# Eleven weight blocks widened in eleven chosen attention turns and five in the first dense batch; the last two token tiles finished in turn

## The chip, the cores and the metric

The kernel runs on one core of a Trainium2 chip. The metric is the device time of one execution in microseconds (us); a run's figure is the median of several executions. The engines are TensorE (PE, with its weight loads listed as PEld), VectorE (DVE), ScalarE (ACT), GpSimd (POOL) and SyncE (SP). SP issues nearly all DMA transfers, in the order of its queue.

## What is computed

An attention with a learned relative bias, then a mixing layer (two Fourier transforms), a normalization and a feed-forward layer with a residual. Shapes: 4 batches, 8 heads, 576 positions, head size 64; model size 512, hidden size 2048.

```python
scores = scale * np.matmul(q, k.transpose(0, 1, 3, 2)) + bias     # bias from a small MLP on |i - j|
attn = softmax(scores)
x = np.matmul(attn, v)                      # (4, 576, 512) after the heads are joined
mixed = np.real(np.fft.fft(np.fft.fft(x, axis=1), axis=2))
u = x + mixed
un = (u - mean(u)) / np.sqrt(var(u) + 1e-6)
out = u + np.maximum(un @ w_ch1, 0.0) @ w_ch2   # w_ch1: 512 x 2048, w_ch2: 2048 x 512
```

`w_ch1` and `w_ch2` arrive as 64-bit floats, seen by the kernel as 64-bit integers (`m1`, `m2`). The kernel makes them 32-bit itself.

## The kernel before

**Stages.** First the bias table is computed and kept in DRAM (0 to about 66 us). Then come 16 units of attention, each a pair of heads of one batch, `n = 4 * pair + batch`. Unit n's steps are spread over the loop's turn n and its neighbours, by the written orders `SECOND` (turn 1) and `ORDER` (turns 0 and 2 to 14). The last turn, 15, runs in the written order `TAIL` together with the mixing and normalization of batch 0. In these stages PE, DVE and ACT execute in the written order (each scope of `manual_schedule` keeps its own order); POOL and SP are ordered by the scheduler's simulation. Then follow four dense batches of four token tiles each, and a last one with the two tiles that hold the leftover positions (`rest_tiles`). In the dense batches the simulation orders everything, but for DVE in the first, whose written order is held.

**A turn.** In the orders, S is a block of scores on PE, D the addition of the bias and the row's extreme on DVE (line 292), X the exponential on ACT (line 307), T a transpose on PE into one of two PSUM buffers (line 451), VT or vT its evacuation to `pt` on ACT or DVE (lines 431, 433), A the product with the values on PE (line 472; five for each unit). W0 to W3 and U0 to U3 are the steps that widen a block of `m1` and one of `m2`.

**Widening** (`widen`, lines 153 to 166). A block is 512 x 128 of `m1` or 128 x 512 of `m2`: 512 KB in 64 bits. Its transfer into `raw` is issued when the tile is made. Step 0 is an ACT copy with a scale (line 162), steps 1 to 3 are a mask and two shift-and-or on DVE (lines 163 to 165). Step 3 is followed by a store of the 256 KB result to DRAM (`w1_d`, `w2_d`; lines 562 and 563). `raw` of `m1` is in pool `rawp`, that of `m2` in `rawu`, one buffer each, so a block's transfer can begin when the block before it is done.

**Which block when.** `weights(n)` widens block n of both matrices in turn n, for n = 1 to 15. Block 0 is widened in eight quarter pieces of 128 x 128 (`first_weights`, pool `rawx`) in turns 4 to 11.

**Transfers around it.** SP also issues, for each turn, `kT` and `qT` two units ahead (line 188), `v` two units ahead (line 195), and in the turn before a new pair of heads (n = 3, 7, 11) the bias of the next pair (line 238, issued from `largest`).

**A dense batch** (`dense`). For each of 16 hidden blocks f: `layer(f)` splits the weights into two fp32r parts (high on ACT, low on POOL; lines 932 and 933), runs `up(f)` on PE (12 matmuls into `hp`), then the ReLU's high part `hh` on ACT (line 972) and its low part `hl` on DVE (line 973). `down(f - 1)` adds the products of `hh`, `hl` and the parts of `w2` to the accumulators `acc` (12 matmuls with four tiles; line 989). `w2_load(f)` (line 952) loads `w2_d[f]` into one of two buffers in each batch; the 16 tiles of `w1` are loaded once, in the first batch, and stay. `run` merges several lists of pieces by their relative position, `(i + 0.5) / len`. In the first batch `main` has 27 pieces (layers 2 to 15, and downs 1 to 13 between them) and `pcs`, the mixing and normalization of batch 1, has 41. `end` adds each tile's accumulator to it on DVE (line 995) and stores it (`store`, lines 1059 and 1115).

Of the kernel before, what the change touches and what calls it, by code (L numbers as in the profile page):

```python
# [9 lines left out]
F32 = mybir.dt.float32  # L10
# [9 lines left out]
DM, FF, HID = 512, 2048, 32  # L20
P = 128
# [5 lines left out]
NF = FF // P  # L27
# [4 lines left out]
HB = {"d": 8, "a": 6}  # L32
WHO = "ddda"

FIRST = range(4, 12)
NEED = [0, 1, 3, 2]
N0 = 572
NT0 = N0 + S
# [92 lines left out]
def body(ctx, tc, a, out):  # L131
    nc = tc.nc
# [16 lines left out]
    w2_d = dram.tile([NF, P, DM], F32, name="w2_d")  # L149
# [264 lines left out]
    with ExitStack() as st:  # L414
# [1 line left out]
        otp = pool("otp", 2, stack=late, side="right")  # L416
        prp = pool("prp", 2, stack=late, side="right")
        rawu = pool("rawu", 1, stack=late, side="right")
        rawx = pool("rawx", 1, stack=late, side="right")
        tps = pool("tps", 2, PSUM, stack=st)  # L420
        ops = pool("ops", 1, PSUM, stack=st)
        score_ps = ExitStack()
# [117 lines left out]
        def turn_of(n, between):  # L540

            for i, w in enumerate(SECOND if n == 1 else ORDER):
                w, u = w.rstrip("'"), n - w.count("'")
                if w[0] in "WU":
                    if n:
                        wd(w)
                elif 0 <= u < U and (u or n == 1 or w[0] not in "SDX"):
                    steps[w[0]](u, w)
                for piece in between.pop(i, ()):
                    piece()  # L550
            assert not between
# [17 lines left out]
                    todo[4]()  # L569
            return step  # L570

        def first_weights(i):

            c = slice(P * (i % 4), P * (i % 4) + P)
            wf = rawx.tile([P, P], F32, tag="wf", name="wx")
            if i < 4:
                res = widen(a["m1"][c, 0:P], wf, [P, P], rawx)
                dst = w1_d[0][:, i]
            else:
                res = widen(a["m2"][0:P, c], wf, [P, P], rawx)  # L580
                dst = w2_d[0][:, c]
            last = res.pop()

            def end():
                last()
                nc.sync.dma_start(dst, wf)
            return res + [end]

        for n in range(U - 1):
            pr = prep(n + 1) if n else []  # L590
            if n:
                wd = weights(n)
            between = {4 + 8 * i: [piece] for i, piece in enumerate(pr)}
            if n in FIRST:
                for i, piece in zip((10, 30, 40, 50), first_weights(FIRST.index(n))):
                    between[i] = [piece]
            turn_of(n, between)
            if n + 2 < U:
                load(n + 2)
            if n == 0:  # L600
                while later:
                    keep_bias()
                x = xp.tile([P, B, 5, DM], F32, tag="x", name="x")
            if n == 6:
                fs = tabp.tile([P, 3, 2, 2, NK], F32R, tag="tab", name="fs")
                nc.gpsimd.tensor_copy(fs[0:1, 0, 0, 0, 0:1], vt[6][0:1, 0, 0:1])
                nc.gpsimd.dma_start(fs, a["fs"])
# [210 lines left out]
            return ut, across, high, low  # L818

        n = U - 1  # L820
        wd = weights(n)
        mix = Mix(0)
        tl = [x[:, 0, t] for t in range(4)]
        un, stats, root, scale = norm(tl)
# [93 lines left out]
        wsp = pool("wsp", 2, stack=st)  # L918
        fgp = pool("fgp", 1, stack=st)
        w1p = pool("w1p", 1, stack=st)  # L920
        hp_ = pool("hhp", 3, stack=st)
        w2p = pool("w2p", 2, stack=st)
        w1 = [w1p.tile([P, 4 * P], F32, name=f"w1_{i}") for i in range(NF)]
        w1 = w1[6:] + w1[:6]
# [11 lines left out]
        def dense(ut, tiles, store, n_first=0, mix=None):  # L936
# [45 lines left out]
                up(f)  # L982
                relu_parts(f)

            def down(f):
                h, w = hs.pop(f), w2s.pop(f)
                for t in range(n):
                    for k, (i, j) in enumerate(PROD):
                        nc.tensor.matmul(  # L989
                            acc[t], h[i][:, P * t:P * t + P], w[j],  # L990
                            start=f == 0 and k == 0, stop=f == NF - 1 and k == 2)

            def end():
                for t in range(n):
                    nc.vector.tensor_tensor(tiles[t], acc[t], tiles[t], ALU.add)
                    store(t)

            if n_first:
                for f in range(1, NF):
                    w1_load(f)  # L1000
                    if f < 3:
                        w2_load(f - 1)
                w1_load(0)
                part = lambda i: mix.fold(nc.vector, 0, i)
                for step, i in (
                        (w1_parts, 1), (part, 0), (part, 1), (relu_parts, 0), (w2_parts, 0), (part, 2),
                        (mix.fold_hi, 0), (w1_parts, 2), (up, 1), (mix.fold_lo, 0), (relu_parts, 1), (w2_parts, 1),
                        (down, 0)):
                    step(i)
                fixed.close()  # L1010
            pieces = []
            for f in range(n_first, NF):
                pieces.append(lambda f=f: layer(f))
                if 0 < f < NF - 1:
                    pieces.append(lambda f=f: down(f - 1))
            return pieces, [lambda: down(NF - 2), lambda: down(NF - 1)], end

        def run(*streams):
            order = []
# [22 lines left out]
        for b in range(B):  # L1042
# [8 lines left out]
            with ExitStack() as held:  # L1051
                if b == 0:
                    held.enter_context(tc.manual_schedule(engines={DVE_}))
                run(main, pcs)
            run(fl + last_down)
            end()

# [2 lines left out]

        main, last_down, end = dense(ut, rest_tiles, store)
        run(main)
        run(last_down)
        end()


def host_layout(inputs):
# [52 lines left out]
```

## Time and profile before

| | |
|---|---|
| median of 3 runs | 777.1 us (773.5 to 778.18) |
| profiled execution | 776.84 us, of which the span from first to last instruction is 775.1 us |
| mean granted TensorE clock | 0.998 |
| PE | 750.3 us busy, 97% of the span |
| DVE | 433.8 us, 56% |
| ACT | 435.2 us, 56% |
| POOL | 340.6 us, 44% |
| DMA | 103.49 MB moved, 134 GB/s on average |

Busy time is the time between the starts and ends of an engine's instructions; matmuls overlap, and their ends are modelled. An idle time in front of an instruction carries the name of what ended it. The chain of waits is followed back from the last instruction, at each step to what released it. Times in rows are us from the start of the span, unless a column says ns.

### The profile page before, as it was taken

What the parts mean: (1) busy time and instruction counts of PE and PEld (TensorE: products, weight loads), DVE (VectorE), ACT (ScalarE), POOL (GpSimd) and SP (SyncE); (2) the same over time, 40 slices, a digit from 0 to 9 for tenths busy, and PEclk for the clock granted to TensorE, in tenths of its full rate; (3) what the DMA queues carried; (4) which work ended last, traced back from release to release, by engine and by line L of the source; (5) the groups of instructions that cost most, each with busy time, mean ns of one, the idle gap of its engine ahead of it and who ended that gap; (6) DMA issues with size and microseconds to landing.
All of it is one profiled execution on the core that took longest, in us unless ns stands there. A gap on an engine that the chain in (4) does not pass through costs nothing.

```text
span 775.1 us, 13211 instructions
## 1 busy us (share of the span) xinstructions
PE 750.3 (97%) x4779; PEld 614.0 (79%) x4779; DVE 433.8 (56%) x968; ACT 435.2 (56%) x901; POOL 340.6 (44%) x290
## 2 busy tenths in 40 slices
PE   6999898999999999999999999999999999999997
PEld 4567686878777887878888888888888888888896
DVE  7997786887788787892843623513137141111443
ACT  7996886878888888653432433334333343333453
POOL 0003555564455663125455434544355444444442
PEclk9999999999999999999999999999999999999999
DMA  8988989989979862244211211122111222111332
GB/s 218 240 225 228 256 234 258 285 238 263 269 196 240 258 187 96 64 154 168 52 35 51 94 43 41 41 55 87 50 41 41 55 75 62 55 41 55 123 96 68
DMA packets 59793, 103.49 MB, mean 134 GB/s; under 512 B 8944, under 2 KB 29040, under 8 KB 58608
## 3 DMA queue, kind: packets, MB, share of 16 engines
q1 hardware_dynamic: 58976, 99.25, 45.5%
q0 software_dynamic: 288, 3.08, 1.3%
q8 instruction: 37, 0.61, 0.3%
q10 hardware_dynamic: 464, 0.33, 0.1%
q14 instruction: 28, 0.23, 0.1%
HBM read 78.90 MB, written 21.07 MB: 129 GB/s over the span
## 4 chain that ended last, share of the span: by engine, by line
PE 85%; DMA 5%; DVE 4%; ACT 4%; issue 1%; ACTq 0%; DVEq 0%; SPq 0%
PE acc L989 25%; PE hp L964 25%; PE s L271 10%; PE o L472 9%; PE t L451 6%; PE bps L400 3%; PE zp L684 2%; DMA raw<-m 2%; DMA bias<-ring 2%; PE abp L704 1%; DVE p L292 1%; ACT p L307 1%; PE ut L807 1%; DMA v<-v 1%; DVE hd L380 1%
## 5 line engine op out<-in xcount | busy, mean ns | idle before, releaser
L973 DVE SCALAR_TENSOR_TENSOR hl<-hp,hh 128x512 fp32r<-128x512 f32 (+1 forms) x80 | 50.9, 636 | 231.6 <-ACT hh L972 231.6
L964 PE MATMUL hp<-tok,w1h 128*128 128x512 f32 (+1 forms) x632 | 179.6, 368 | 0.0
L933 POOL TENSOR_TENSOR w1l<-w,w1h 128x512 fp32r<-128x512 f32 x79 | 103.1, 1305 | 111.9 <-ACT w1h L932 110.7
L964 PEld LDWEIGHTS hp<-tok,w1h 128*128 128x128 f32 x632 | 115.0, 188 | 20.1
L933 POOL TENSOR_TENSOR w2l<-w2f,w2h 128x512 fp32r<-128x512 f32 x64 | 84.1, 1315 | 106.5 <-ACT w2h L932 106.3
L292 DVE CUSTOM_DVE_ANT_0 p<-s,bias 128x576 f32<-128x576 f32 x128 | 95.3, 753 | 39.4 <-PE s L271 35.9
L964 PE MATMUL hp<-tok,w1l 128*128 128x512 f32 (+1 forms) x316 | 116.1, 368 | 0.0
L932 ACT ACTIVATE w2h<-w2f 128x512 fp32r<-128x512 f32 x80 | 50.5, 631 | 116.5 <-POOL w1l L933 79.7
L989 PE MATMUL acc<-w2h,hh 128*128 128x512 f32 x288 | 112.4, 390 | 0.0
L989 PE MATMUL acc<-w2l,hh 128*128 128x512 f32 x288 | 112.4, 390 | 0.0
L932 ACT ACTIVATE w1h<-w 128x512 fp32r<-128x512 f32 x79 | 49.8, 631 | 111.3 <-PE hp L964 102.8
L989 PE MATMUL acc<-w2h,hl 128*128 128x512 f32 x288 | 107.6, 391 | 0.0
L271 PE MATMUL s<-kh,qs 128*128 128x288 f32 (+1 forms) x320 | 98.3, 326 | 4.0 <-DVE nm L292 3.9
L307 ACT ACTIVATE p<-p,nm 128x576 f32<-128x576 f32 x128 | 98.0, 771 | 1.4 <-DVE nm L292 1.4
L431 ACT ACTIVATE pt<-t 128x512 f32<-128x512 f32 x141 | 77.6, 594 | 32.6 <-PE t L451 19.5
L271 PE MATMUL s<-kl,qs 128*128 128x288 f32 (+1 forms) x320 | 88.2, 295 | 0.9 <-DVE kl L212 0.9
L451 PE MATMUL t<-ident,p 128*128 128x128 f32 x576 | 79.1, 273 | 6.5 <-ACT pt L431 6.5
L208 POOL TENSOR_SCALAR kh<-kT 128x576 fp32r<-128x576 f32 (+1 forms) x28 | 22.4, 819 | 141.5 <-PE s L271 113.7
L472 PE MATMUL o<-pt,v 128*64 128x288 f32 x640 | 84.2, 411 | 0.0
L271 PEld LDWEIGHTS s<-kh,qs 128*128 128x128 f32 (+1 forms) x320 | 58.5, 183 | 20.7 <-issue 7.0
L451 PEld LDWEIGHTS t<-ident,p 128*128 128x128 f32 x576 | 66.2, 140 | 8.1 <-ACT pt L431 7.7
L472 PEld LDWEIGHTS o<-pt,v 128*64 128x64 f32 x640 | 43.3, 137 | 30.7 <-issue 4.7
(149 smaller groups left out, 1276.2 us busy)
## 6 DMA issues: line engine op xcount, KB each, us to landing
w2f<-w_d SPq DMA_DIRECT2D x80, 256.0 KB, 2.7
raw<-m SPq DMA_DIRECT2D x30, 512.0 KB, 5.5
kT<-kT SPq DMA_DIRECT2D x32, 304.0 KB, 5.7
qT<-qT SPq DMA_DIRECT2D x32, 288.0 KB, 5.0
bias_d<-ring SPq DMA_DIRECT2D x54, 144.0 KB, 2.7
bias<-bias_d SPq DMA_DIRECT2D x24, 288.0 KB, 6.1
v<-v SPq DMA_DIRECT2D x16, 320.0 KB, 7.0
out<-x SPq DMA_DIRECT2D x18, 256.0 KB, 3.2
```

Source lines behind the costliest of these rows:

```text
L271: nc.tensor.matmul(ps[:m, c, :CH], qs[:, c0:c0 + m], kk[:, k0 + c * CH:k0 + (c + 1) * CH], start=k == 0, stop=k == 1, skip_group_check=True)
L292: nc.vector.tensor_tensor_reduce(p, bank.pop((n, i))[:, :, :CH], bias, -0.125, 3.0e38, ALU.add, ALU.min, nms[n][:, blk:blk + 1])
L307: nc.scalar.activation(p, p, AF.Exp, bias=nms[n][:, blk:blk + 1], scale=-1.0, accum_out=sums[n][:, blk:blk + 1])
L400: nc.tensor.matmul(ps[32 * t4:32 * t4 + 32, c, :CH], w2[:, int(rev)], h[:, c * CH:(c + 1) * CH], start=True, stop=True, tile_position=(0, ...
L431: nc.scalar.activation(dst, src, AF.Copy)
L451: nc.tensor.transpose(tp[:, 128 * t:128 * t + 128], pb[t].rearrange("p h s -> p (h s)")[:, k0:k0 + 128], ident)
L472: nc.tensor.matmul(os_[u][e, c, :CH], vt[u][:, j, e], pts[u][:, 2 * j + h if j < 4 else 8, c * CH:(c + 1) * CH], start=j == 0, stop=j == 4 ...
L932: nc.scalar.activation(h, src, AF.Copy)
L933: eng.tensor_tensor(l, src, h.bitcast(F32), ALU.subtract)
L964: nc.tensor.matmul(ps[:, :N], w[wi][:, P * kb:P * kb + P], ut[ui][:, kb, :N], start=i == 0, stop=i == len(mm) - 1)
L973: nc.vector.scalar_tensor_tensor(hl[:, :N], ps[:, :N], 0.0, hh[:, :N].bitcast(F32), ALU.max, ALU.subtract)
L989: nc.tensor.matmul(acc[t], h[i][:, P * t:P * t + P], w[j], start=f == 0 and k == 0, stop=f == NF - 1 and k == 2)
```

## The change

- Eleven blocks (0 to 10) are widened in turns 2, 3, 5, 6, 7, 9, 10, 11, 13, 14 and 15: turn n takes block `WIDE.index(n)`. Turns 1, 4, 8 and 12 have no weight work. `first_weights` and its pool go.
- Blocks 11 to 15 are widened in the first dense batch by `widen_rest`: ten half blocks, each of four pieces (start the transfer; ACT copy and mask; shift-and-or; shift-and-or, and for `m2` the store to `w2_d`), merged into the batch as a third list of 44 places (40 pieces and four empty ones at its end). The transfers of the first two half blocks come first; half block k + 2 starts when half block k is done. An `m1` block is widened straight into its `w1` tile, so that no store and no load are needed for it.
- The pool of `hh` and `hl` has two buffers instead of three; a pool `rawd` for the `m2` blocks is new.
- In the last batch, the two hidden blocks at the end are applied to tile 0 first, which is added and stored, and then to tile 1.

```diff
--- before.py
+++ after.py
@@ -32,7 +32,7 @@
 HB = {"d": 8, "a": 6}
 WHO = "ddda"
 
-FIRST = range(4, 12)
+WIDE = [2, 3, 5, 6, 7, 9, 10, 11, 13, 14, 15]
 NEED = [0, 1, 3, 2]
 N0 = 572
 NT0 = N0 + S
@@ -416,7 +416,6 @@
         otp = pool("otp", 2, stack=late, side="right")
         prp = pool("prp", 2, stack=late, side="right")
         rawu = pool("rawu", 1, stack=late, side="right")
-        rawx = pool("rawx", 1, stack=late, side="right")
         tps = pool("tps", 2, PSUM, stack=st)
         ops = pool("ops", 1, PSUM, stack=st)
         score_ps = ExitStack()
@@ -542,7 +541,7 @@
             for i, w in enumerate(SECOND if n == 1 else ORDER):
                 w, u = w.rstrip("'"), n - w.count("'")
                 if w[0] in "WU":
-                    if n:
+                    if n in WIDE:
                         wd(w)
                 elif 0 <= u < U and (u or n == 1 or w[0] not in "SDX"):
                     steps[w[0]](u, w)
@@ -569,31 +568,11 @@
                     todo[4]()
             return step
 
-        def first_weights(i):
-
-            c = slice(P * (i % 4), P * (i % 4) + P)
-            wf = rawx.tile([P, P], F32, tag="wf", name="wx")
-            if i < 4:
-                res = widen(a["m1"][c, 0:P], wf, [P, P], rawx)
-                dst = w1_d[0][:, i]
-            else:
-                res = widen(a["m2"][0:P, c], wf, [P, P], rawx)
-                dst = w2_d[0][:, c]
-            last = res.pop()
-
-            def end():
-                last()
-                nc.sync.dma_start(dst, wf)
-            return res + [end]
-
         for n in range(U - 1):
             pr = prep(n + 1) if n else []
-            if n:
-                wd = weights(n)
+            if n in WIDE:
+                wd = weights(WIDE.index(n))
             between = {4 + 8 * i: [piece] for i, piece in enumerate(pr)}
-            if n in FIRST:
-                for i, piece in zip((10, 30, 40, 50), first_weights(FIRST.index(n))):
-                    between[i] = [piece]
             turn_of(n, between)
             if n + 2 < U:
                 load(n + 2)
@@ -818,7 +797,7 @@
             return ut, across, high, low
 
         n = U - 1
-        wd = weights(n)
+        wd = weights(WIDE.index(n))
         mix = Mix(0)
         tl = [x[:, 0, t] for t in range(4)]
         un, stats, root, scale = norm(tl)
@@ -918,7 +897,8 @@
         wsp = pool("wsp", 2, stack=st)
         fgp = pool("fgp", 1, stack=st)
         w1p = pool("w1p", 1, stack=st)
-        hp_ = pool("hhp", 3, stack=st)
+        hp_ = pool("hhp", 2, stack=st)
+        rawd = pool("rawd", 1, stack=st)
         w2p = pool("w2p", 2, stack=st)
         w1 = [w1p.tile([P, 4 * P], F32, name=f"w1_{i}") for i in range(NF)]
         w1 = w1[6:] + w1[:6]
@@ -982,21 +962,21 @@
                 up(f)
                 relu_parts(f)
 
-            def down(f):
-                h, w = hs.pop(f), w2s.pop(f)
-                for t in range(n):
+            def down(f, tiles=None):
+                h, w = hs[f], w2s[f]
+                for t in range(n) if tiles is None else tiles:
                     for k, (i, j) in enumerate(PROD):
                         nc.tensor.matmul(
                             acc[t], h[i][:, P * t:P * t + P], w[j],
                             start=f == 0 and k == 0, stop=f == NF - 1 and k == 2)
 
-            def end():
-                for t in range(n):
+            def end(which=None):
+                for t in range(n) if which is None else which:
                     nc.vector.tensor_tensor(tiles[t], acc[t], tiles[t], ALU.add)
                     store(t)
 
             if n_first:
-                for f in range(1, NF):
+                for f in range(1, len(WIDE)):
                     w1_load(f)
                     if f < 3:
                         w2_load(f - 1)
@@ -1013,7 +993,37 @@
                 pieces.append(lambda f=f: layer(f))
                 if 0 < f < NF - 1:
                     pieces.append(lambda f=f: down(f - 1))
+            if n == 2:
+                return pieces, [lambda t=t, f=f: down(f, [t]) for t in range(2) for f in (NF - 2, NF - 1)], end
             return pieces, [lambda: down(NF - 2), lambda: down(NF - 1)], end
+
+        def widen_rest():
+
+            chunks = []
+            for f in range(len(WIDE), NF):
+                chunks.append(chunk(
+                    a["m1"][:, P * f:P * f + P].rearrange("(k p) c -> p k c", p=P), [P, 4, P], w1[f], f, rawp))
+                chunks.append(chunk(a["m2"][P * f:P * f + P], [P, DM], None, f, rawd))
+            res = [chunks[0].pop(0), chunks[1].pop(0)]
+            for k, c in enumerate(chunks):
+                res += c + [b.pop(0) for b in chunks[k + 2:k + 3]]
+            return res
+
+        def chunk(src, shape, dst, f, rp):
+            todo = []
+
+            def start():
+                wf = rp.tile([P, DM], F32, tag="wf", name="wf") if dst is None else dst
+                todo.extend(widen(src, wf, shape, rp))
+                if dst is None:
+                    todo.append(lambda: nc.sync.dma_start(w2_d[f], wf))
+
+            def step(*which):
+                for i in which:
+                    if i < len(todo):
+                        todo[i]()
+
+            return [start, lambda: step(0, 1), lambda: step(2), lambda: step(3, 4)]
 
         def run(*streams):
             order = []
@@ -1051,7 +1061,10 @@
             with ExitStack() as held:
                 if b == 0:
                     held.enter_context(tc.manual_schedule(engines={DVE_}))
-                run(main, pcs)
+                    wide = widen_rest()
+                    run(main, pcs, wide + [lambda: None] * (len(wide) // 10))
+                else:
+                    run(main, pcs)
             run(fl + last_down)
             end()
 
@@ -1060,8 +1073,9 @@
 
         main, last_down, end = dense(ut, rest_tiles, store)
         run(main)
-        run(last_down)
-        end()
+        for t in range(2):
+            run(last_down[2 * t:2 * t + 2])
+            end([t])
 
 
 def host_layout(inputs):
```

## Rows read from the trace of the kernel before

**Rows 1.** Windows, first dense batch: us, then each engine's busy us, PEclk, DMA share, GB/s
```profile
346.00:437.00 91.00, 91.00 (x436) 76.72 (x435) 45.09 (x78) 35.06 (x70) 47.37 (x38) 1.00 0.26 79
```

**Rows 2.** Timeline of PE: start, us, instruction; in brackets idle time before, what ended it
```profile
81.56 1.15 PE L451 MATMUL t<-ident,p 128*128 128x128 f32 x8 [2.50 <-ACT pt L431]
...
132.15 1.14 PE L451 MATMUL t<-ident,p 128*128 128x128 f32 x8 [2.48 <-ACT pt L431]
...
158.16 0.40 PE L271 MATMUL s<-kh,qs 128*128 128x288 f32 x1 [0.91 <-DVE nm L292]
...
198.88 1.14 PE L451 MATMUL t<-ident,p 128*128 128x128 f32 x8 [0.94 <-ACT pt L431]
```

**Rows 3.** The chain of waits in order of time: start, us, what
```profile
73.41 5.63 DMA raw<-m
...
114.45 4.03 PE o L472 x32
121.12 8.45 DMA raw<-m
133.29 4.03 PE o L472 x32
...
182.73 4.03 PE o L472 x32
190.80 6.09 DMA v<-v
200.02 4.03 PE o L472 x32
...
248.28 4.03 PE o L472 x32
...
280.46 4.03 PE o L472 x32
```

**Rows 4.** Timeline of ACT, turns 1 and 8
```profile
79.06 0.66 ACT L162 ACTIVATE uf<-raw 128x512 f32<-128x512 f32 x1 [3.86 <-DMA raw<-m]
...
196.35 0.68 ACT L162 ACTIVATE uf<-raw 128x512 f32<-128x512 f32 x1 [1.99 <-DMA raw<-m]
```

**Rows 5.** Groups by line and shape, 66 to 300 us: count, busy us, mean ns, idle before
```profile
L164 DVE SCALAR_TENSOR_TENSOR raw<-raw 128x512 int32<-128x512 int32 x28 | 23.1, 823 | 0.5
L163 DVE TENSOR_SCALAR raw<-raw 128x512 int32<-128x512 int32 x28 | 14.2, 506 | 9.0 <-ACT wf L162 9.0
L165 DVE SCALAR_TENSOR_TENSOR uf<-uf,raw 128x512 int32<-128x512 int32 x14 | 12.2, 868 | 0.5
...
L162 ACT ACTIVATE wf<-raw 128x512 f32<-128x512 f32 x14 | 9.3, 666 | 0.0
```

**Rows 6.** Timelines of DVE and PE in the first dense batch
```profile
363.49 0.69 DVE L973 SCALAR_TENSOR_TENSOR hl<-hp,hh 128x512 fp32r<-128x512 f32 x1 [3.22 <-ACT hh L972]
...
389.78 0.68 DVE L973 SCALAR_TENSOR_TENSOR hl<-hp,hh 128x512 fp32r<-128x512 f32 x1
...
367.81 0.39 PE L989 MATMUL acc<-w2h,hh 128*128 128x512 f32 x1
...
392.71 0.39 PE L989 MATMUL acc<-w2h,hh 128*128 128x512 f32 x1
```

**Rows 7.** Waits of SP's queue, 345 to 437 us: us in total, times, longest
```profile
SPq L952 <- POOL w2l L933: 73.8, 15, 6.8
```

**Rows 8.** DMA issues: count, KB, median us to landing; whole run, then 115 to 135 us
```profile
raw<-m SPq DMA_DIRECT2D x30, 512.0 KB, 5.5
...
raw<-m SPq DMA_DIRECT2D x3, 512.0 KB, 8.1
```

**Rows 9.** Timeline of the end, DVE and SP's queue
```profile
769.47 1.29 DVE L995 TENSOR_TENSOR x<-acc,x 128x512 f32<-128x512 f32 x2 [1.68 <-PE acc L989]
770.18 0.94 SPq L1059 DMA_DIRECT2D out<-x  x2
```

**Rows 10.** Line 933, 345 to 440 us: ns least/median/most, first and last start, form
```profile
L933 POOL TENSOR_TENSOR w2l<-w2f,w2h x17: 1282/1292/1987, 347.6 to 439.5; 128x512 fp32r<-128x512 f32 x17
```

## The prediction

> **What bounds the kernel now.** I read the row of busy time by stage first. In the first dense batch (346 to 437 us) TensorE is busy for all 91 us, while DVE is busy for 45.09, ACT for 35.06 and POOL for 47.37 [rows 1]. That stage, and the three batches behind it, are one unbroken stream of matmuls: nothing that ACT, DVE or POOL do there costs time until it makes TensorE wait.
>
> The attention stage comes before it, and there I looked for the rows of TensorE that have idle time in front. From 75 to 300 us there are six; the four longest are shown [rows 2]: 2.50, 2.48 and 0.94 us, each ended by ACT's copy of transposed scores, and 0.91 us ended by DVE. The other two are under 0.5 us each, and the change does not touch them.
>
> The chain of work says what that costs. A run of 32 `o` matmuls straddles the end of every turn, so the distance from one run to the next is a turn. Five turns (9 to 13) take 280.46 - 200.02 = 80.44 us, 16.09 us each. Turn 4 takes 133.29 - 114.45 = 18.84 us, 2.75 more; turn 8 takes 200.02 - 182.73 = 17.29 us, 1.20 more [rows 3]. The idle times there are 2.48 and 0.94 us, so a stall costs about 0.27 us beyond its idle row. In the same chain the weight transfers `raw` hold up the stall of turn 1 (5.63 us from 73.41) and of turn 4 (8.45 us from 121.12), and a transfer of `v`, issued just behind one, that of turn 8 (6.09 us from 190.80) [rows 3].
>
> ACT's rows close it: in turns 1 and 8 it sat for 3.86 and 1.99 us before the copy that opens a block (`uf<-raw`), waiting for `raw<-m` [rows 4]; turn 4 has the same picture. ACT works in order, so the exponentials and the evacuations behind that copy waited too, and TensorE ran out of free transpose banks. These are turns 1, 4 and 8; in turns 4 and 8 the queue also carries the bias of the next pair of heads.
>
> **The change part by part.**
>
> *Blocks leave turns 1, 4, 8 and 12.* With no weight copy in those turns, ACT has nothing there that waits for `raw`. Turn 4 should fall by 2.75 us and turn 8 by 1.20 us to 16.09. Turn 1's order of work differs, so I take its idle row plus the same 0.27: 2.77 us. Turn 12 shows no stall: 0. Sum 6.72 us. What is late next? The buffers of `raw` come free at the same moments as before, so the transfers for turns 2, 5 and 9 can start where those for turns 1, 4 and 8 did and have a turn more to land; `kT` and `v` then wait behind no more than before. I count no new wait; the price if one appears is a rival.
>
> *The eight quarter pieces of block 0 go from turns 4 to 11.* They take DVE, ACT and queue work out of turns that TensorE bounds. The five turns of 16.09 us hold three with such a piece (9 to 11) and two without (12, 13) [rows 3]; 248.28 - 200.02 and 280.46 - 248.28 both give 16.09 a turn. Worth 0. The 0.91 us of turn 6 [rows 2] come from DVE: two operations on a small column that belong to the tail's order were run in that turn. The change does not move them, so I leave that stall; the bounds are 0 and, by its turn's excess, 1.2 us of gain.
>
> *Five blocks go into the first dense batch.* Ten half blocks, each one ACT copy of 666 ns, one mask of 506 ns and two shift-and-or of 823 and 868 ns on DVE [rows 5]. Added: 10 x 0.67 = 6.7 us of ACT and 10 x 2.20 = 22.0 us of DVE. DVE goes from 45.1 to 67.1 and ACT from 35.1 to 41.8 of 91 us [rows 1]. Neither fills. The cover for single delays is the time between `hl` (the low part of the hidden layer) and the `acc` matmul run that needs it: 364.18 to 367.81 is 3.63 us, and the tightest steady case, 390.46 to 392.71, is 2.25 us [rows 6]. The pieces come one at a time, three to a layer, each under 0.9 us; alone they fit.
>
> The danger is DVE's fixed order in this batch. A mask that stands ahead of an `hl` waits for its ACT copy, the copy for its transfer, and `hl` and all the folds wait behind it. By the interleaving rule, a half block's transfer is issued five of 44 places ahead of its mask: 5 / 44 x 91 = 10.3 us. Against that: SP's queue is in order, and a `w2f` load at its head waits for POOL, 73.8 us in 15 waits, 4.9 on average and 6.8 at most [rows 7]; then `raw` takes 5.5 us to land (median of 30), 8.1 in the crowded turn 4 [rows 8]. Typical: 4.9 + 5.5 = 10.4, in balance with 10.3 and inside the 2.25 of cover. Worst: 6.8 + 8.1 = 14.9, over 12.6 by 2.3 us. The DMA engines are busy for 0.26 of this stage [rows 1], not crowded, so I take the typical end: 0 us, with 0 to 2.3 us for each of eight half blocks (the first two start early) as bounds. The 15 added transfers less five `w1` loads also stand in SP's queue; their issues are well under a microsecond each and come out of its waiting.
>
> *Hidden-layer buffers from three to two.* `up(f)` comes after `down(f-2)` on TensorE, so the buffer that the ReLU of layer f takes is free before its input exists: 0. If the scheduler put a ReLU ahead of that matmul, it would cost up to one `down`, 2.7 us, once for each batch.
>
> *The last two token tiles in turn.* Before, both final additions run after the last matmul, 769.47 to 770.76, and the second store follows the second one [rows 9]. Afterwards the first addition runs under the six matmuls of the other tile. What goes is the second's half of the 1.29 us, 0.65 us. The two issues take 0.94 us [rows 9], so the bounds are 0.3 (a first-tile product that waits for `hl`) and 0.94. I take 0.65.
>
> *POOL beside the added work.* POOL's `w2l` takes 1.29 us in the median of this stage and 1.99 us at the longest [rows 10], so something holds it up now and then. The Trainium skill (SBUF — State Buffer, "SBUF: two separate sides") says that a DVE operation with two SBUF inputs and a GpSimd operation that reads SBUF exclude each other for a whole instruction. The row agrees in direction. By that rule each of the 20 added shift-and-or operations could hold POOL for its full length; rival 3 gives what that would cost.
>
> **Sum.** 6.72 + 0.65 = 7.37 us off the profiled execution's 776.84 us: 769.5 us. The median before is 777.1, so the profiled execution stands for it within 0.3 us. One per cent, about what a measurement of this kernel can tell from no change, is 7.8 us: the bound lies at 769.3, almost on the forecast.
>
> **Rivals.**
> 1. *The transfers come late in the dense batch.* For: a queue whose head nearly always waits, and a fixed DVE order. Against: the balance above and idle DMA engines. One to three half blocks at about 2 us: 771.5 to 776.
> 2. *Slower.* The same mechanism on every half block, at the worst: 8 x 2.3 = 18.4 us, 788 us. It passes 1% slower (784.9) when each of the eight lands more than 1.9 us beyond the cover, 14.5 us after its buffer came free. Against it: it needs the longest queue wait and turn 4's landing time at once, each time.
> 3. *DVE shuts POOL out.* Each of the 20 added operations (0.85 us on average [rows 5]) holds POOL up for its length: 17 us, and 786.5 us if POOL had no slack. Against: POOL is busy for 47.37 of 91 us [rows 1], and 47.4 + 17 = 64 still leaves 27 us.
> 4. *A stall moves instead of going.* `kT`, `v` or a bias part is the next to be late in turn 4 or 8. For: the DMA engines stay crowded there, `raw` still taking 8.1 us to land [rows 8]. Half of 3.95 us comes back: 771.5.
> 5. *More gain.* Turn 6's 1.2 us goes too, or the end saves 0.94: 768 to 768.5.
>
> **How the numbers follow.** Forecast (stalls gone, batch hides the work) 0.60; rival 1 0.13; rival 2 0.05; rival 3 0.03; rival 4 0.07; rival 5 0.12. Rivals 2 and 3 hold the 0.08 for slower by over 1%. The forecast's case straddles the bound at 769.3, a little more of it above than below: 0.26 of its 0.60 counts as faster, and with rival 5 that is 0.38. The rest, 0.54, is within 1%. The range reaches down to rival 5 with a us for the spread of runs, 766.8, and up to most of rival 1, 775. The forecast's own range is 768.3 to 771.
>
> **What would show it.** In the profile after, right: the idle rows at turns 1, 4 and 8 are gone, those runs of `o` lie 16.1 us apart, the dense stage from its first matmul to its last is as long as before, and one addition stands after the last matmul. Wrong: idle rows on TensorE between 346 and 440 us; `hl` waiting for a mask that waits for `raw` (rivals 1 and 2); `w1l` or `w2l` well over 1.3 us with TensorE waiting for POOL (rival 3); an idle row in turn 4 or 8 ended by another transfer (rival 4).

## The result and the profile after

The kernel after takes 779.71 us in the median (777.77 to 782.89), the kernel before, run beside it, 775.3 us (773.5 to 779.57). The ratio is 1.0055, with an interval of 1.0039 to 1.0071. The change makes the kernel 0.55% slower: no difference by the bound of one per cent, yet on the other side of the forecast and above the range. The profiled execution is one of the slower ones of after, 781.77 us at a mean granted clock of 0.992; the three of the 17 at 0.999 or above took 777.77 to 778.46 us.

The profiled execution of after has a span of 779.8 us, 4.7 us more than before. I split it at the first `hp` matmul (line 863 after, 884 before) and at the last two `acc` matmuls (line 969, before 989): up to the first it is the attention with its tail, between the two the five dense batches.

| profiled execution | first `hp` | last two `acc` | dense stage |
|---|---|---|---|
| before | 343.26 | 769.04 | 425.78 |
| after | 339.43 | 774.98 | 435.55 |

The attention got 3.83 us shorter and the dense stage 9.77 us longer.

**Attention.** On TensorE's timeline after, the idle rows of turns 1, 4 and 8 [rows 2] are gone, and the runs of `o` around turn 4 lie 16.10 us apart where they lay 18.84 apart [rows 3]:

```profile
114.08 4.10 PE L471 MATMUL o<-pt,v 128*64 128x288 f32 x32
...
130.18 4.10 PE L471 MATMUL o<-pt,v 128*64 128x288 f32 x32
...
155.39 0.40 PE L271 MATMUL s<-kh,qs 128*128 128x288 f32 x1 [1.19 <-DVE nm L292]
```

The last row is turn 6's stall, left as forecast (1.19 us for 0.91). Nearly all that this profile lacks of the forecast 6.72 us it lost ahead of turn 1: an idle row of 1.55 us at 66.5 us (0.59 before), and behind it a granted TensorE clock of 0.52 and 0.63 from 68 to 72 us. Such a row comes and goes with the same work: it is 1.44 us in a kernel with the attention of before, and 0.52 to 1.87 us in the kernels with that of after. So it belongs to a run, not to the change.

**First dense batch.** The row of busy time by stage, as in [rows 1] (us; then PE, PEld, DVE, ACT, POOL; granted clock, DMA share, GB/s):

```profile
346.00:437.00 91.00, 87.56 (x403) 72.84 (x403) 64.30 (x98) 33.80 (x70) 46.11 (x35) 0.98 0.35 115
```

TensorE, busy for all 91 us before, is now busy for 87.56. DVE has 64.30 us, near the 67.1 of the sum, and ACT not even as much as before: neither is full. The waits view from 380 to 445 us (who waited for whom: us in total, times, longest) names whom TensorE waited for:

```profile
PE acc L969 <- ACT hh L952: 4.2, 2, 2.2
...
PE acc L969 <- DVE hl L953: 1.5, 1, 1.5
```

These are three idle rows: 1.46 us at 391.6, 1.97 at 418.2 and 2.20 at 442.8. ACT's timeline shows the copies that waited and what stood ahead of the last two `hh` (the high part of the hidden layer, line 952); the copy at 364.82 comes up again further below:

```profile
364.82 0.66 ACT L162 ACTIVATE w<-raw 128x512 f32<-128x512 f32 x1 [2.70 <-DMA raw<-m]
...
391.72 0.66 ACT L162 ACTIVATE wf<-raw 128x512 f32<-128x512 f32 x1 [4.99 <-DMA raw<-m]
...
399.82 0.69 ACT L162 ACTIVATE w<-raw 128x512 f32<-128x512 f32 x1 [4.87 <-DMA raw<-m]
...
407.21 0.66 ACT L162 ACTIVATE wf<-raw 128x512 f32<-128x512 f32 x1 [4.90 <-DMA raw<-m]
...
416.51 0.66 ACT L162 ACTIVATE w<-raw 128x512 f32<-128x512 f32 x1 [6.84 <-DMA raw<-m]
417.07 0.61 ACT L912 ACTIVATE w1h<-w 128x512 fp32r<-128x512 f32 x1
417.59 0.58 ACT L952 ACTIVATE hh<-hp 128x512 fp32r<-128x512 f32 x1
...
441.08 0.63 ACT L912 ACTIVATE w2h<-w2f 128x512 fp32r<-128x512 f32 x1 [6.30 <-DMA w2f<-w_d]
441.61 0.61 ACT L912 ACTIVATE w1h<-w 128x512 fp32r<-128x512 f32 x1
442.13 0.58 ACT L952 ACTIVATE hh<-hp 128x512 fp32r<-128x512 f32 x1
```

ACT waits at eight of the ten copies, 2.70 to 6.84 us each, and every one of these eight starts when its transfer lands. Behind the copy at 416.51 stand `w1h` and `hh`, then DVE's `hl`, then TensorE. The copy's transfer shows why it was late (SP's queue, then DVE's rows: an `hl`, the release of the buffer, the next `hl`):

```profile
412.71 0.38 SPq L160 DMA_DIRECT2D raw<-m  x1
...
408.91 0.69 DVE L953 SCALAR_TENSOR_TENSOR hl<-hp,hh 128x512 fp32r<-128x512 f32 x1 [4.46 <-ACT hh L952]
...
412.00 0.68 DVE L165 SCALAR_TENSOR_TENSOR w<-w,raw 128x512 int32<-128x512 int32 x1
418.20 0.69 DVE L953 SCALAR_TENSOR_TENSOR hl<-hp,hh 128x512 fp32r<-128x512 f32 x1 [5.52 <-ACT hh L952]
```

The transfer could be issued only when DVE had let go of the buffer, at 412.7. ACT had been at the copy since 416.51 - 6.84 = 409.67, 3 us before the issue. The transfer itself took 3.8 us, the median of the nine issued from 338 us on. DVE was late with the buffer because its `hl` at 408.91 had waited 4.46 us for the `hh` behind the copy at 407.21: a late copy makes the next transfer late too. The third stall has one more link: block 15 of `m2` is stored at 436.24 and loaded again from 438.28, and the `w2h` that waits for it stands ahead of `hh`. Counted from the first `hp`, that store comes at 96.81 us here and at 88.92 us in the kernel below with only two transfers: it comes late because DVE's work does by then.

Behind two of the stalls TensorE's clock fell too (2-us windows, columns as above):

```profile
416.00:418.00 2.00, 0.25 (x2) 0.00 (x0) 0.00 (x0) 1.49 (x3) 0.24 (x1) 1.00 0.20 76
418.00:420.00 2.00, 1.78 (x7) 1.46 (x8) 1.76 (x3) 1.70 (x4) 2.00 (x2) 0.91 0.00 0
420.00:422.00 2.00, 2.00 (x6) 1.51 (x6) 2.00 (x4) 0.00 (x0) 0.98 (x2) 0.50 0.00 0
422.00:424.00 2.00, 2.00 (x8) 1.62 (x7) 1.99 (x4) 0.64 (x1) 1.85 (x3) 0.74 0.19 69
```

0.50 is the lower of the two levels, 1.2 GHz. The missing clock of these windows is 2 x (0.09 + 0.50 + 0.26) = 1.70 us of work, and the third stall's windows give as much (0.88, 0.50, 0.76: 1.72). Idle 5.63 and clock 3.42 make 9.05 of the 9.77 us.

**The end.** The additions stand where they stood [rows 9]:

```profile
774.98 0.61 PE L969 MATMUL acc<-w2h,hl 128*128 128x512 f32 x2
775.40 1.29 DVE L975 TENSOR_TENSOR x<-acc,x 128x512 f32<-128x512 f32 x2 [1.68 <-PE acc L969]
776.12 0.94 SPq L1072 DMA_DIRECT2D out<-x  x2
```

The edit wrote the products tile by tile, but PE is not held to the written order in that batch, and the scheduler ran the last matmuls of both tiles in the old order.

### The profile page after: what moved, and what is told of

Its sections match the earlier page's. It is cut to its first block, busy times and chain, and to the rows that moved or that the text cites. A ratio compares the mean times of both kernels' runs of the same rounds, so it can differ in the third digit from the quotient of the medians.

```text
span 779.8 us, 13166 instructions
## 1 busy us (share of the span) xinstructions
PE 754.9 (97%) x4779; PEld 617.1 (79%) x4779; DVE 441.7 (57%) x950; ACT 434.8 (56%) x895; POOL 339.8 (44%) x290
## 5 line engine op out<-in xcount | busy, mean ns | idle before, releaser
L913 POOL TENSOR_TENSOR w2l<-w2f,w2h 128x512 fp32r<-128x512 f32 x64 | 86.0, 1343 | 108.2 <-ACT w2h L912 108.1
L208 POOL TENSOR_SCALAR kh<-kT 128x576 fp32r<-128x576 f32 (+1 forms) x28 | 20.6, 752 | 142.5 <-DMA bias_d<-ring 72.0
```

The costliest lines, as they stand in the source:

```text
L208: nc.gpsimd.tensor_scalar(dst[:, c], src[:, c], 1.0, 0.0, ALU.mult, ALU.add)
L913: eng.tensor_tensor(l, src, h.bitcast(F32), ALU.subtract)
```

## The experiments

Diffs are against the kernel after unless said otherwise. "Dense stage" is measured as in the table above. The kernel before took 775.2 to 775.6 us in all these comparisons.

### Taking the widening out of the batch, part by part

**No widening in the batch.**

```diff
-                    run(main, pcs, wide + [lambda: None] * (len(wide) // 10))
+                    run(main, pcs)
```

with all 16 blocks of both matrices loaded, from blocks `f % 11`.

> The changed kernel without the widening in the first dense batch: blocks 11 to 15 are not made at all, and the 32-bit blocks 0 to 4 are loaded a second time in their place, so the output is not the reference's. Attention, hidden-layer buffers and the end stay as changed. Theory T (the ACT copies of the half blocks stand in ACT's queue ahead of the ReLU's high part and wait there for transfers that are issued too late): the dense stage falls from 435.9 us back to the 426.2 us of before, and the time from 779.7 to about 770. Rival L (DVE has too much work in that batch): the same here, since that work is gone too. Rival B (the two hidden-layer buffers, or something in the attention, cost it): the dense stage stays several us above 426, the time above 775.

Measured: 768.95 us, ratio 0.9926 (0.9898 to 0.9955); first `hp` 335.88, dense stage 425.76 us, that of before, with two buffers for `hh` and `hl`. The attention edit alone is worth 6.2 us in the medians and 7.4 in the profile, where turn 6's stall happens to be missing. The chain of waits has 14 runs of `o`; ten of the 13 distances between them are 16.06 to 16.14 us, turn 4 among them (16.09); turn 8 takes 16.25 us:

```profile
112.04 4.03 PE o L471 x32
128.13 4.03 PE o L471 x32
...
176.44 4.03 PE o L471 x32
192.69 4.03 PE o L471 x32
```

**No ACT copy.**

```diff
-            return [start, lambda: step(0, 1), lambda: step(2), lambda: step(3, 4)]
+            return [start, lambda: step(1), lambda: step(2), lambda: step(3, 4)]
```

(the last shift-and-or reads the masked words in place of the copy's; not shown)

> The changed kernel without the ACT copy of the ten half blocks in the dense batch; the last shift-and-or reads the masked words in its place, so blocks 11 to 15 are wrong. Transfers, stores and all three DVE operations stay. Theory T: nothing on ACT waits for a transfer, so the waits for the ReLU's high part (4.2 us of idle on TensorE, and the drops of its clock that follow) go; what is left is what DVE's own waits cost: 771 to 775. Rival L: DVE does the same work, the time stays at 778 to 780.

Measured: 771.47 us, ratio 0.9945 (0.9921 to 0.9968); dense stage 427.02 us with one idle row, 0.97 us at 389 behind `hl`, and full clock.

**Two transfers instead of ten.** The first two half blocks are transferred, the other eight work on the same buffers.

```diff
-        raw = rp.tile(shape, I64, tag="raw", name="raw")
+        raw = kept.get(rp) if kept else None
+        if raw is None: ...   # tile and transfer, once for each pool
```

> The changed kernel in which only the first two half blocks of the dense batch are transferred; the other eight go through all their ACT, DVE and store work on the words that lie in the buffers, so blocks 12 to 15 are wrong. Theory T: no copy waits for a transfer, 770 to 772. Rival L: the work on DVE and ACT is all there, 777 to 780.

Measured: 769.03 us, ratio 0.9924 (0.9899 to 0.9948); dense stage 426.06 us. The same stretch as above:

```profile
346.00:437.00 91.00, 91.00 (x438) 76.56 (x437) 67.83 (x106) 38.58 (x76) 47.02 (x37) 1.00 0.23 70
```

All the widening work is there, DVE even 3.5 us busier than after, and TensorE is busy for all 91 us. So it is not the work; the transfers are needed for every one of the three stalls, also for the one that `hl` ends. This kernel takes away their traffic together with the waiting for them; the kernel without the ACT copy has all ten transfers and yet neither of the stalls that `hh` ends, so what those two need is ACT waiting for a transfer.

**The ten half blocks on top of the kernel before** (its attention and its buffers of block 0 untouched; `hhp` with two buffers, `rawd` and `widen_rest` added).

> The kernel before, with all its widening in the attention, and in the first dense batch the changed kernel's ten half blocks on top (blocks 11 to 15 are made twice), with its pools. If the dense batch alone carries the loss, about 775.3 + 9.8 = 785 us, whatever theory holds in the batch; if the loss comes from the two parts together, or from the attention, it stays under 780.

Measured: 782.66 us, ratio 1.0099 (1.0061 to 1.0136); dense stage 434.08 us with idle rows of 1.38 (`hl`), 2.14 and 2.27 us (`hh`) in the same places and one of 0.83 us (`hl`) at 439. The dense part alone brings a loss of 8.30 us in its stage; the time lies 2.3 us under the 785 expected.

### Moving the copy, the end of the list, ACT's order

**Copy on DVE.**

```diff
-            lambda: nc.scalar.activation(dst, hi.bitcast(F32), AF.Copy, scale=2.0 ** -112),
+            lambda: nc.vector.tensor_scalar(dst, hi.bitcast(F32), 2.0 ** -112, None, ALU.mult),
```

(in the dense batch only; the same with `nc.gpsimd` in the next one)

> The kernel after, with the scaling copy of the ten half blocks of the first dense batch done by DVE instead of ACT (one multiplication more on DVE for each, about 0.5 us by the shift-and-or rows; ten make 5 us of the 91). Theory T (the copies hold up ACT's order, and with it the high part of the hidden layer): ACT is free, and DVE, which waits for the mask anyway, waits as it did without any copy: 770 to 772.5 us, no idle row on TensorE ended by ACT, no lost clock in the dense stage, below the kernel before. Rival Q (any in-order engine that takes the copy gives the wait to TensorE, since the low part and the folds stand behind it on DVE): 777 us or more, with idle rows ended by DVE's low part.

Measured: 777.89 us, ratio 1.0031 (1.0014 to 1.0049). My theory missed by 5 us, and rival Q had the time, though not the instruction that ends the row. ACT's stall at 418 us is gone and one of 0.94 us is left at 441, but TensorE stood for 3.88 us before 391.28, ended by a fold of DVE (`z11l`), and its clock fell to 0.50 for about 6 us. DVE's rows from 380 to 396 us are back to back: folds of the mixing, widening and `hl`, without one idle time. In this stretch DVE has no room. The one copy that DVE does between 380 us and that fold takes 0.42 us, so its length does not explain 3.88 us. TensorE's order differs: here one `acc` matmul stands between the last `hp` and the product of that fold, in after there are eight. That this order is the rest of the 3.88 us was not tested.

**Copy on GpSimd.**

> The kernel after, with the copy of the ten half blocks of the first dense batch done by GpSimd. Theory T: ACT is free; GpSimd was busy for about half of this batch and its low parts of the weights have slack of some us, so 769 to 773 us. Rival Q: the wait of 3 to 5 us for a transfer now stands ahead of a low part of the weights (w1l, w2l), TensorE's idle rows are ended by POOL, and the time is 775 us or more.

Measured: 772.59 us, ratio 0.9967 (0.9945 to 0.999); dense stage 429.75 us, idle rows 2.10 us (`hl`, 390) and 1.31 us (`hh` behind the load of block 15, 436). This lies within the theory's 769 to 773.

**An earlier end of the list.**

```diff
-                    run(main, pcs, wide + [lambda: None] * (len(wide) // 10))
+                    run(main, pcs, wide + [lambda: None] * (len(wide) // 2))
```

> The kernel after, with 20 empty places at the end of the third list instead of 4: the widening ends at two thirds of the batch instead of nine tenths, and a transfer has fewer other pieces between its start and its copy. Theory T: less time for each transfer, so the copies wait longer on ACT and TensorE has at least as many idle rows: 779 to 786 us. Rival E (it is the late end: block 15 of the second matrix goes through a store and a load just before it is needed): that stall goes, and the time falls by what it costs with its lost clock, about 4 us, to 775 or 776 us.

Measured: 771.05 us, ratio 0.9941 (0.9919 to 0.9962). My expectation was wrong in direction, and the rival's too small. Five places between a transfer's start and its copy are 7.6 us here instead of 10.3, and ACT's waits did not get longer: 25.3 us in 8 against 35.9 in 9 (waits view, from 340 to 445 us; of after, then of this kernel).

```profile
ACT w L162 <- DMA raw<-m: 18.6, 4, 6.8
ACT wf L162 <- DMA raw<-m: 17.3, 5, 5.0
```
```profile
ACT wf L162 <- DMA raw<-m: 13.8, 4, 5.9
ACT w L162 <- DMA raw<-m: 11.5, 4, 3.6
```

So the lead by places says nothing about ACT's waits, and not every wait of ACT costs time: by these rows it counts which `hh` a copy stands ahead of. With the copies over by 409 us the stalls of 418 and 443 us are gone, two short ones are left (0.78 us by `hl` at 388, 1.25 by `hh` at 402), the clock stays at 1.00, and the dense stage takes 429.01 us.

**ACT held to the written order.**

```diff
-                    held.enter_context(tc.manual_schedule(engines={DVE_}))
+                    held.enter_context(tc.manual_schedule(engines={DVE_, ACT_}))
```

> The kernel after, with ACT as well as DVE held to the written order in the first dense batch. In the kernel after, ACT reached each copy of a half block before its transfer had landed, twice before it was even issued: the scheduler orders ACT by its own simulation. Theory O (the lead by written places exists, and the scheduler's order of ACT threw it away): the copies wait little, the high part of the hidden layer is in time, TensorE's idle rows ended by ACT between 380 and 440 us go but for the one of the last block's store and load (442 us), and the time is 771 to 774 us. Rival D (the transfers are issued late because DVE frees the buffers late, and ACT's order does not matter): waits of 3 to 5 us on ACT stay and the time is 777 us or more.

Measured: 792.85 us, ratio 1.024 (1.0198 to 1.0282). The theory's mechanism holds and its price does not. No instruction of ACT waits for `raw` any more: the lead by places was there, and the scheduler's order of ACT had used it up. But the written order puts `hh` where TensorE always waits for it, and `w1h` behind it (ACT, then TensorE):

```profile
410.07 0.60 ACT L952 ACTIVATE hh<-hp 128x512 fp32r<-128x512 f32 x1 [4.98 <-PE hp L944]
410.56 0.38 ACT L687 ACTIVATE bs<-abp 128x257 f32<-128x257 f32 x1
410.83 0.67 ACT L162 ACTIVATE w<-raw 128x512 f32<-128x512 f32 x1
```
```profile
418.64 0.50 PE L969 MATMUL acc<-w2h,hh 128*128 128x512 f32 x1 [0.69 <-ACT hh L952]
...
425.06 0.50 PE L969 MATMUL acc<-w2h,hh 128*128 128x512 f32 x1 [0.69 <-ACT hh L952]
```

0.7 to 1.0 us in front of nearly every `down`, and further rows for `w1h` and `w1l`. In this batch the scheduler's freedom on ACT is worth more than the copies' waits cost.

### The end, and a version that beats both

**The end held.**

```diff
-        for t in range(2):
-            run(last_down[2 * t:2 * t + 2])
-            end([t])
+        with tc.manual_schedule(engines={PE_}):
+            for t in range(2):
+                run(last_down[2 * t:2 * t + 2])
+                end([t])
```

> The kernel after, with TensorE held to the written order for the last two tiles, so that all products of tile 0 come before those of tile 1 (in the kernel after the scheduler put them back into the old order). Theory (the end edit is worth 0.65 us once TensorE follows it): 0.6 us less than the kernel after, 779.1 us, with one addition behind the last matmul. Rival (DVE's order keeps both additions at the end): no difference, two additions behind the last matmul. The time alone will hardly tell; the rows will.

Measured: 778.19 us, ratio 1.0034 (1.0019 to 1.005), against 1.0055 (1.0039 to 1.0071) of after; the intervals overlap, so the rows have to tell. Now one addition stands behind the last matmul, and from the start of the last matmul to the end of the last addition it is 771.98 - 770.86 = 1.12 us, where it was 776.69 - 775.20 = 1.49 us in after (its last matmul starts 0.22 us behind the row's 774.98):

```profile
770.86 0.39 PE L969 MATMUL acc<-w2h,hl 128*128 128x512 f32 x1
771.29 0.69 DVE L975 TENSOR_TENSOR x<-acc,x 128x512 f32<-128x512 f32 x1 [0.70 <-PE acc L969]
```

This profile has the three dense stalls of after (1.32, 1.75, 2.25 us, and 0.86 at 434) with the clock at 1.00 throughout, and a dense stage of 433.70 us.

**Earlier end of the list and end held.**

> The kernel after with the earlier end of the list (which gave a ratio of 0.9941 to the kernel before) and TensorE held to the written order for the last two tiles. Theory E (one addition and its store no longer stand behind the last matmul, nothing else changes): 0.3 to 0.9 us below it, ratio 0.993 to 0.994. Rival H (the hold costs: the scheduler plans the whole last batch another way): 0.996 or more.

Measured: 770.34 us, ratio 0.9929 (0.9906 to 0.9952): the best complete version, 4.8 us below before and 9.4 below after, and the hold shows no cost. The step from 0.9941 lies inside both intervals, so its own gain is not told by the times.

**Twelve blocks in the attention, four in the batch.** `WIDE` gets turn 12; earlier end of the list.

> Earlier end of the list, twelve blocks in the attention and four in the dense batch, no hold at the end. Theory E: as with the hold (0.9967) or up to 0.9 us above, 0.9965 to 0.998, because the two half blocks fewer move the waits in the batch and do not remove the one near 388 us. Rival H (the hold was what cost): 0.993 to 0.9945.

Measured: 774.01 us, ratio 0.9984 (0.9969 to 1.0). Turn 12 costs nothing (16.09 us, as counted). But with fewer pieces in the same batch they lie elsewhere: TensorE waits 2.34 us for `hl` at 389.85, and the clock falls behind it:

```profile
390.00:392.00 2.00, 2.00 (x11) 1.82 (x12) 1.97 (x4) 0.16 (x1) 2.00 (x2) 0.79 0.00 0
392.00:394.00 2.00, 2.00 (x6) 1.60 (x6) 1.69 (x3) 0.00 (x0) 0.20 (x1) 0.50 0.07 12
394.00:396.00 2.00, 2.00 (x9) 1.55 (x8) 0.00 (x0) 0.00 (x0) 0.00 (x0) 0.85 0.94 312
```

The same with the end held:

> Twelve blocks in the attention (turn 12, which showed no stall, takes one again), four in the first dense batch with as many empty places at the end of the list as half of its pieces, and TensorE held to the written order at the end. Theory: the kernel with the earlier end took 771.05 us with five blocks; two half blocks fewer take one more wait away (about 1 us) and the end gives 0.6: 769 to 770.5 us. Rival (turn 12 stalls once a transfer is in it): an idle row on TensorE in turn 12 and 771.5 us or more.

Measured: 772.49 us, 0.9967 (0.995 to 0.9983), with 2.24 us at 387.5. GpSimd copies, earlier end and hold together:

> Five blocks in the first dense batch with the earlier end of the list, their copies on GpSimd instead of ACT, and the end held. Theory: the earlier end takes away the stall behind the last store (1.31 us in the run with copies on GpSimd), GpSimd the one behind ACT (1.25 us in the run with the earlier end), the end gives 0.6: 769.5 to 770.5 us. Rival (GpSimd's waits move the low parts of the weights): 772 us or more, idle rows ended by POOL.

Measured: 774.89 us, 0.9995 (0.9978 to 1.0012), with four short idle rows between 388 and 409 us. And with turn 12 as well:

> All of it: twelve blocks in the attention, four in the dense batch, copies on GpSimd, earlier end of the list, TensorE held at the end. Theory: 769 to 770 us, near the 768.95 of the kernel without any widening in the batch. Rival (turn 12 stalls, or GpSimd's waits count): 771.5 us or more.

Measured: 773.22 us, 0.998 (0.9953 to 1.0008), with one of 2.51 us at 388.8. None of these last three came to the 769 to 770.5 us that their theories gave. So on top of the earlier end neither less to widen nor a freer ACT gained anything: in each of these four the longest idle row of the batch stands at 387 to 390 us and is ended by `hl`, 1.61 to 2.51 us; the version with the earlier end and the hold has none there.

## Why the prediction was wrong

**Right: the attention.** 6.72 us of stalls in turns 1, 4 and 8 were forecast to go and nothing to take their place. The idle rows that ACT's copies ended went in all kernels with this edit, turns 4 and 8 of after run in 16.1 us, and the kernel without widening in the batch is 6.2 us below before. Turn 12, the quarter pieces and the two hidden-layer buffers were rightly priced at 0. Rival 4 did not occur in the profile of after, but it did in others with the same attention, most in that with the copy on DVE, where a transfer of the bias is late in turns 4 and 8 (DVE, then TensorE):

```profile
124.19 0.76 DVE L293 CUSTOM_DVE_ANT_0 p<-s,bias 128x576 f32<-128x576 f32 x1 [1.98 <-DMA bias<-bias_d]
```
```profile
125.01 0.40 PE L272 MATMUL s<-kh,qs 128*128 128x288 f32 x1 [1.45 <-DVE nm L293]
...
190.47 0.40 PE L272 MATMUL s<-kh,qs 128*128 128x288 f32 x1 [0.76 <-DVE nm L293]
```

So "I count no new wait" holds in some executions only.

**Wrong: to whom the lead of 10.3 us was given, and so "I take the typical end: 0 us".** This is the step that decided. The 10.3 us were counted in written places, from a transfer's issue to its mask on DVE, and there they were: in after the nine masks start 7.5 to 15.5 us behind the issue, 11.4 on average, and none of them waits. What was set against them was even too large: seven of the eight later transfers were issued within about 0.4 us of the buffer's release (2.7 us once) where 4.9 had been counted, and they landed in 3.8 us for 5.5. But the copy between transfer and mask is ACT's. Only DVE follows the places in that batch; the scheduler orders ACT, and ACT reached eight of the copies between 3.0 us before the issue and 1.4 us behind it. The copy that starts at 416.51 was reached at 409.67, before the issue at 412.71, and DVE wanted it only for this mask:

```profile
425.16 1.42 DVE L163 TENSOR_SCALAR raw<-raw 128x512 int32<-128x512 int32 x1
```

With ACT held (792.85 us) no copy waits. So the prediction looked for the damage on the wrong engine: it asked what a mask holds up on DVE, and the wait stood on ACT, ahead of `hh`. Rival 1 came nearest (late transfers, though by way of DVE's order) and priced one to three half blocks at 2 us; it was three stalls of 1.46 to 2.20 us, which by its rule would be 769.5 + 5.6 = 775.1 us.

**Too small: what a stall costs.** In the attention a stall cost 0.27 us beyond its idle row [rows 2, 3], and I carried no more than that to the dense batch. There the clock fell behind two of three: the stage lost 9.77 us for 5.63 us of idle rows in this execution, and about 7.9 us for 6.4 in that with the end held, where the clock did not fall.

**Too small: the cover.** 2.25 us from `hl` to its use is a cover for one delay. DVE's added work was near its term, 25.4 us for 22.0 (groups by line and shape, 340 to 440 us: count, busy us, mean ns, idle before):

```profile
L164 DVE SCALAR_TENSOR_TENSOR raw<-raw 128x512 int32<-128x512 int32 x10 | 8.3, 832 | 0.1
L163 DVE TENSOR_SCALAR raw<-raw 128x512 int32<-128x512 int32 x10 | 6.8, 677 | 0.0
L165 DVE SCALAR_TENSOR_TENSOR wf<-wf,raw 128x512 int32<-128x512 int32 x5 | 5.9, 1174 | 0.0
L165 DVE SCALAR_TENSOR_TENSOR w<-w,raw 128x512 int32<-128x512 int32 x5 | 4.4, 872 | 0.0
```

But from 366.5 to 393 us DVE's rows, folds and widening, follow each other without idle time (26.20 us busy of 26.50). The `hl` at its start waited for an `hh` behind ACT's copy at 364.82, and the `hl` at 390.88 is the one of the stall at 391.6. In after, then with two transfers:

```profile
366.52 0.69 DVE L953 SCALAR_TENSOR_TENSOR hl<-hp,hh 128x512 fp32r<-128x512 f32 x1 [3.54 <-ACT hh L952]
...
390.88 0.68 DVE L953 SCALAR_TENSOR_TENSOR hl<-hp,hh 128x512 fp32r<-128x512 f32 x1
```
```profile
362.09 0.69 DVE L957 SCALAR_TENSOR_TENSOR hl<-hp,hh 128x512 fp32r<-128x512 f32 x1 [1.93 <-ACT hh L956]
...
386.37 0.68 DVE L957 SCALAR_TENSOR_TENSOR hl<-hp,hh 128x512 fp32r<-128x512 f32 x1
```

Counted from the first `hp` (339.43 and 336.38), the first is 1.38 us later in after and the second 1.46 us, the length of the idle row. So it takes both: a late start, and a stretch with no room to catch up.

**Wrong: the end, 0.65 us.** The new order was only written, and the scheduler put the matmuls back; the prediction never asked who orders that stage. The size was too large as well: with PE held the rows give 1.49 - 1.12 = 0.37 us, near the lower bound of 0.3, because the first addition runs partly beside the last matmul in the old order too (it starts at 775.40, the last matmul ends at 775.59).

**Rivals 2 and 3.** Rival 2's price of 2.3 us on every half block did not come: eight copies waited, and three stalls came of it. POOL's `w2l` did get slower (345 to 440 us: a median of 1.47 us against 1.29 before [rows 10], a mean of 1.49 against 1.36), but TensorE waited for it nowhere from 380 to 445 us, so rival 3 as forecast had no part in it. DVE paid the other way: in its full stretch five operations take 1.40 to 1.79 us where others of their form take 0.42 to 0.69, and each ends 0.3 to 0.6 us behind a POOL operation that began before it, like this pair:

```profile
378.70 1.74 POOL L913 TENSOR_TENSOR w1l<-w,w1h 128x512 fp32r<-128x512 f32 x1
```
```profile
379.32 1.40 DVE L656 TENSOR_TENSOR gh<-ge,gh 64x256 fp32r<-64x256 f32 x1
```

Together that is some 5 us of the 26 (an estimate from these rows). The kernel with two transfers has such rows too, so they do not make the stall, but they take the room to catch up. The Trainium skill's rule on the two sides (SBUF — State Buffer, "SBUF: two separate sides"), that whichever starts first blocks the other for the whole instruction, agrees with these rows.

**Left open.** Why the same stretch gives a stall of 0.8 us in one version and 2.5 in another was not followed further than to DVE's full stretch and the places of the pieces in it, nor was the run-to-run difference at 66 us. What the store and load of block 15 cost by itself was not separated from the delays ahead of it.

## What to carry to other kernels

A lead counted in the written order holds only on engines that are held to that order: ask for every engine in the chain who orders it, and what stands in its queue behind the instruction that will wait. A delay is absorbed by the slack at its place, not by an engine's mean idle share: here a full stretch of 26 us on an engine busy for 64.30 of 91 us passed it on. And an edit that only rewrites the order of a stage which a scheduler orders may change nothing.

## What was not expected of the hardware

TensorE's clock fell to 0.50, its lower level, for some microseconds behind idle rows of 1.97 and 2.20 us (after), 2.34 us (twelve blocks) and 3.88 us (copy on DVE); behind the first three the missing clock is 1.7 us of work each. Behind the idle row of 1.55 us at 66.5 us in after it was 0.52 on average from 68 to 70 us. Behind idle rows of 2.25, 2.24 and 2.51 us in three other profiles (end held; twelve blocks with the end held; all together) it stayed at 1.00, and the first of these has the first dense batch of after unchanged. So the length of the idle row alone does not tell it; what else does, the runs do not show.
